# Linear attention and a gated MLP on one core: query features turned on VectorE, numerators for a whole batch as sixteen array tiles, front and order set anew

## The chip, the cores and the metric

The kernel runs on one core of one Trainium2 chip. The metric is the device time of one execution in microseconds (us). The engines of the core are TensorE (PE in the profile; PEld is its weight load), VectorE (DVE), ScalarE (ACT), GpSimd (POOL) and SyncE (SP), which only issues DMAs here.

## What is computed

Four batches of 1088 tokens, 4 heads of 32. `phi` makes 64 features from two projections onto 8 directions each; attention is linear in these features; its output, 128 values a token, goes through a two-layer MLP of width 2048.

```python
a, b = einsum('rd,bhsd->bhsr', S1, x), einsum('rd,bhsd->bhsr', S2, x)    # phi(x):
phi = einsum('bhsi,bhsj->bhsij', a, b).reshape(..., 64)
q_p, k_p = phi(q), phi(k)
kv = einsum('bhsf,bhsd->bhfd', k_p, v);  z = sum(k_p, axis=2)
num = einsum('bhsf,bhfd->bhsd', q_p, kv)
den = einsum('bhsf,bhf->bhs', q_p, z)[..., None] + 1e-06
x = (num / den) as [4352 tokens, 128]
h = x @ w_in                                   # 128 -> 2048
g = where(h >= 1, h, where(h <= -1, 0, (h + 1) ** 2 / 4))
out = g @ w_out                                # 2048 -> 128
```

## The kernel before, in words

**The MLP.** Tokens lie along the free dimension in 9 chunks of 512 (the last 256); the width of 2048 is cut into 16 blocks of 128. One chunk and one block make a *unit*, 144 in all (0 to 143). Units 0 to 31 weave chunks 0 and 1, four blocks at a time, because the weights still arrive; then each chunk's 16 blocks follow one another; the last two chunks are woven again. Values and weights are split into a rounded part and a rest (`x_hi`, `x_lo`, `wi_hi`, `wi_lo`, ...), so a product is three matmuls. A unit is, in PE, three matmuls into `h` (L619 to L621) and three into `acc` (L655, L656, L659); in ACT the half-square `s` in two passes (L630, L632); in DVE the clamp `g` (L635); then `g_hi`, either as a cast on ACT (L641) or as a second clamp on DVE (L635), by the share `HI_ACT`; and `g_lo`, a subtraction on POOL (L645). The weights come as doubles and are taken apart by `from_double` on ACT, POOL and DVE (`mag`, `hc`, `m`, L366 to L394), 512 columns at a time (`raw_i`, `raw_o`).

**The attention of a batch.** `keys` projects the keys of 9 tiles of 128 tokens (`abk`), copies (`ab`, ACT), multiplies to features (`kp`, DVE; one group on POOL), sums the denominators' vector (`z`, `zm`) and the 64 x 32 sums per head (`kv`), and turns those into `kvb`. `queries` goes in groups of three tiles (batch 0: 2, 2, 3, 2): project with the denominators' vector beside it (`abq`, L521), copy (`as`), `terms`, `den`, its inverse, `ap`, then the features `qp` (L543, DVE). PE turns each tile's features in two transposes of 128 x 128 into a bank `tp` (L553), ACT or DVE copies it to `qpT`, and PE gathers the numerators `nd` (L571) in tiles of 64 rows by 32 columns. `x_hi` and `x_lo` are taken from `nd`. All of these stand beside the units of earlier chunks. Batch 0 is the *front*: unit 0 needs its first four tiles.

**The order.** Every step has a due time, written by hand or by a formula on its unit's number; `Plan.run` plays the steps with estimated costs on in-order engines and a fixed number of buffers (8 PSUM banks, tag `ps`) and writes out one order for each engine. A matmul `warm` fills PE where the plan has nothing for it before time `WARM`. Each engine runs its order as written and waits where an operand is late. DMAs go through SP's queue, and a few through ACT's (`load` with `lands`).

Of the kernel before, what the change touches and what calls it, by code (L numbers as in the profile page):

```python
# [18 lines left out]
P = 128  # L19
# [3 lines left out]
FIRST = 32  # L23
# [5 lines left out]
ND = 0.115  # L29
TP = 0.109  # L30
I0 = -12.0
LATE = 4
Q2 = -4.0
Q3 = -2.0
I1 = 2.0
O1 = 6.0
KP_POOL = (2,)
O0 = -4.0
K_LANDS = (2.6, 3.1)
Q_RATE = 210e3  # L40
KVM = 0.8
LOADS = {1: (-4.0, 0.0, -2.0), 2: (11.0, 13.0, 12.0), 3: (54.0, 58.0, 56.0)}
HI_ACT = (0.8, 0.36)
# [21 lines left out]
class Step:  # L65


    def __init__(self, due, ways):
        self.due, self.ways = due, ways
        self.next = []  # L70
        self.start = self.taken = None
        self.mode = 1


class Plan:
# [3 lines left out]
    AHEAD = 8.0  # L79
    WAIT = 0.45  # L80
    EDGE = 2.0
    SWITCH = 0.095
    STAY = 3.0
# [38 lines left out]
    def run(self):  # L122
# [26 lines left out]
        while left or done:  # L149
# [13 lines left out]
            for e in engines:  # L163
# [51 lines left out]
                if e == "SP":  # L215
# [52 lines left out]
def tile_kernel(ctx: ExitStack, tc: tile.TileContext, qT, kT, v, S, w_in, w_out, outT):  # L268
# [14 lines left out]
                 ap=2, qp=2, qpT=4, kvm=1, kvb=2, zm=1, s=4, g=4, g_hi=6, g_lo=6, o=2)  # L283
# [28 lines left out]
    raw_i0 = Buf("raw", "raw_i0", [P, WC, 2], I32)  # L312
    k0 = Buf("k", "k0", [P, NTL, P])
    nc.gpsimd.memset(of(k0)[:, 3, :1], 0)
# [15 lines left out]
    x_hi = cst.tile([P, NT + 64], F32R, name="x_hi")  # L330
    x_lo = cst.tile([P, NT + 64], F32R, name="x_lo")
# [19 lines left out]
    def from_double(due, raw, raw_tok, n, tag, whole=None, whole_tok=None, hi=None, lo=None, toks=None):  # L351
# [10 lines left out]
        def m():  # L362
# [3 lines left out]
        plan.add(due, "ACT", act(n, False), lambda: nc.scalar.activation(of(mag), hw().bitcast(F32), AF.Abs),  # L366
                 r=[raw_tok], w=[mag])
# [29 lines left out]
    def weights(due, src, c, hi, lo, tag, due_load=None, lands=None):  # L397
        raw = raw_i0 if lands is not None else Buf("raw", f"raw_{tag}{c}", [P, WC, 2], I32)
# [14 lines left out]
    QLOAD = [range(0, 4), range(4, NTL)]  # L413
    QPART = [0, 0, 1, 1]
    loaded = {}

    def load_attn(b, due_k, due_q, due_v):
        kb = Buf("k", f"k{b}", [P, NTL, P]) if b else k0
        qb = Buf("q", f"q{b}", [P, NTL, P])
        vb = Buf("v", f"v{b}", [P, NTL, P])  # L420
        loaded[b] = kb, qb, vb
        for due, t, src in ((due_k, kb, kT), (due_q, qb, qT), (due_v, vb, v)):
            if b:
                load(due, src[b], t, P * NTL * P * 4)
            else:
                for i, grp in enumerate({0: GRP, 1: QLOAD, 2: [range(NTL)]}[[kb, qb, vb].index(t)]):
                    sl = slice(grp[0], grp[-1] + 1)
                    other = t is kb and i
                    load(-50 + i if other else (due if not isinstance(due, list) else due[i]) + 0.1 * i, src[b][:, sl], t,
                         P * len(grp) * P * 4, tok=t.part(i), view=lambda x, sl=sl: x[:, sl], lands=K_LANDS[i - 1] if other else None,  # L430
                         rate=Q_RATE if t is vb else 370e3 if t is qb and i else 190e3)

    def keys(b, d):
# [4 lines left out]
        late = 3.0 if front else 0.0  # L438
# [4 lines left out]
        for gi, grp in enumerate(groups):  # L443
            n = len(grp)
            kt = [kb.part(gi) if front else kb]
# [13 lines left out]
            pool = front and gi in KP_POOL  # L459
# [35 lines left out]
        for gi, grp in enumerate(groups):  # L495
# [3 lines left out]
        kvm = Buf("kvm", f"kvm{b}", [P, 2, F])  # L499
        copy_to(d(KVM) + late, lambda: of(kvm), lambda: of(kv)[:, :F].unsqueeze(1).broadcast_to([P, 2, F]), P, [kv], [kvm])  # L500
        plan.add(d(0.85) + late, "PE", 0.11, lambda: nc.tensor.transpose(
            out=of(kv)[:, P : 2 * P], in_=of(kvm).rearrange("p s f -> p (s f)"), identity=ident), r=[kvm], w=[kv]).mode = 0
        kvb = Buf("kvb", f"kvb{b}", [P, P])
        copy_to(d(0.9) + late, lambda: of(kvb), lambda: of(kv)[:, P : 2 * P], P, [kv], [kvb])
        return kvb

    def queries(b, kvb, dues):
        _, qb, _ = loaded[b]
        front = b == 0
        for gi, grp in enumerate(QGRP[b]):  # L510
# [32 lines left out]
            plan.add(d(0.4), "DVE", dve(m * F), lambda ap=ap, qp=qp, view=view, m=m, n=n: nc.vector.tensor_tensor(  # L543
                out=of(qp)[:, :n].rearrange("p t (h i j) -> p (t h) i j", h=H, i=R),
                in0=of(ap)[:, :m].unsqueeze(3).broadcast_to([P, m, R, R]),
                in1=view()[:, :, 1].unsqueeze(2).broadcast_to([P, m, R, R]), op=ALU.mult), r=[abc, ap], w=[qp])
# [39 lines left out]

    def x_tokens(kind, c0, n):
        out = []
        for b in range(B):
            for gi, grp in enumerate(QGRP[b]):  # L590
                lo = b * SEQ + grp[0] * P
                hi = b * SEQ + min(SEQ, (grp[-1] + 1) * P)
# [16 lines left out]
    AFTER = 3.6  # L609

    def unit(u):
# [14 lines left out]
        late = u >= len(units) - LATE  # L626
# [12 lines left out]
        share = 1.0 if late else HI_ACT[u >= FIRST]  # L639
# [30 lines left out]
    load(-30, S, s_raw, P * SC * 8, tok="s_raw", rate=94e3)  # L670
    load_attn(0, -29, [-28.5, -27], -27.5)
# [14 lines left out]
    kvb = keys(0, lambda f: -16 + 7 * f)  # L686
    queries(0, kvb, [lambda f: -9 + 4 * f, lambda f: -8.5 + 4 * f, lambda f: Q2 + 5 * f, lambda f: Q3 + 5 * f])
# [82 lines left out]
```

## Time and profile before

| | |
|---|---|
| three runs | 248.21 us median (248.18 to 248.82) |
| the profiled execution | 247.75 us, of which the span of instructions is 246.0 us |
| PE, PEld | 97%, 76% busy |
| ACT, DVE, POOL | 85%, 80%, 78% busy |
| chain that ended last | PE 68%, ACT 22%, DMA 3%, DVE 3% |
| TensorE clock granted | full speed throughout |

Read it with the end of the chain in mind: PE carries most of it, and ACT carries it up to about 69 us. A matmul's record overlaps the next one's, so what a matmul costs is read from the start of one to the start of the next.

### The profile page before, as it was taken

The numbers are of one execution on the slowest core, as the hardware profiler recorded it, in microseconds if no ns is written. First come the engines' busy times: TensorE is split into PE (matmuls) and PEld (weight loads), VectorE is DVE, ScalarE is ACT, GpSimd is POOL, SyncE is SP. The second block draws the span as 40 slices with busy tenths as digits, with TensorE's granted clock in tenths as the row PEclk, the third lists the DMA queues.
The fourth block names the chain that finished last, engine by engine and source line by source line (L and its number), as shares of the span: only waits on it lengthen the run. The fifth ranks groups of instructions, "written<-read, shape, count | busy, mean of one in ns | idle before, by whom it ended". The sixth has DMA issues, their size and how long they took to land.

```text
span 246.0 us, 5793 instructions
## 1 busy us (share of the span) xinstructions
PE 237.5 (97%) x2160; PEld 186.7 (76%) x2160; DVE 196.8 (80%) x386; ACT 209.8 (85%) x445; POOL 190.9 (78%) x175
## 2 busy tenths in 40 slices
PE   8699999999999999999999999999999999999994
PEld 3577768777858877878788787788778877888883
DVE  2499997499979767888779968787889799768873
ACT  2358999999998979977996689968996898889993
POOL 4234799999997768896797648895899488979991
PEclk9999999999999999999999999999999999999999
DMA  6972195300020100001000100001000100010001
GB/s 211 408 310 91 42 377 169 156 1 0 3 95 27 63 4 3 0 0 43 3 0 3 45 0 4 1 1 43 3 0 3 43 0 1 3 43 1 0 3 64
DMA packets 4779, 13.93 MB, mean 57 GB/s; under 512 B 528, under 2 KB 1168, under 8 KB 4752
## 3 DMA queue, kind: packets, MB, share of 16 engines
q1 hardware_dynamic: 4320, 12.65, 14.1%
q10 hardware_dynamic: 432, 0.92, 1.0%
q8 instruction: 17, 0.28, 0.5%
q14 instruction: 10, 0.08, 0.1%
HBM read 11.34 MB, written 2.23 MB: 55 GB/s over the span
## 4 chain that ended last, share of the span: by engine, by line
PE 68%; ACT 22%; DMA 3%; DVE 3%; issue 1%; POOL 0%; ACTq 0%; DVEq 0%; POOLq 0%
PE acc L659 11%; PE acc L655 10%; PE acc L656 10%; PE h L619 10%; PE h L621 9%; PE h L620 9%; ACT s L632 7%; ACT s L630 7%; ACT g_hi L641 5%; DMA raw_i<-in_w_in 3%; PE tp L553 2%; PE nd L571 2%; PE abq L521 2%; PE warm L292 1%; DVE g L635 1%
## 5 line engine op out<-in xcount | busy, mean ns | idle before, releaser
L645 POOL TENSOR_TENSOR g_lo<-g,g_hi 128x512 fp32r<-128x512 f32 (+1 forms) x140 | 171.8, 1250 | 34.9 <-DVE g_hi L635 16.2
L635 DVE SCALAR_TENSOR_TENSOR g<-h,s 128x512 f32<-128x512 f32 (+1 forms) x144 | 93.3, 657 | 31.8 <-ACT s L632 24.5
L630 ACT ACTIVATE s<-h 128x512 f32<-128x512 f32 (+1 forms) x144 | 79.8, 585 | 12.1 <-PE h L621 11.4
L632 ACT ACTIVATE s<-s 128x512 f32<-128x512 f32 (+1 forms) x144 | 86.5, 626 | 1.3
L619 PE MATMUL h<-x_hi,wi_hi 128*128 128x512 f32 (+1 forms) x144 | 56.1, 389 | 0.4 <-DVE g_hi L635 0.2
L655 PE MATMUL acc<-g_hi,wo_hi 128*128 128x512 f32 (+1 forms) x144 | 55.4, 386 | 0.1
L621 PE MATMUL h<-x_hi,wi_lo 128*128 128x512 f32 (+1 forms) x144 | 54.6, 379 | 0.0
L620 PE MATMUL h<-x_lo,wi_hi 128*128 128x512 f32 (+1 forms) x144 | 54.5, 379 | 0.0
L656 PE MATMUL acc<-g_hi,wo_lo 128*128 128x512 f32 (+1 forms) x144 | 54.4, 379 | 0.0
L659 PE MATMUL acc<-g_lo,wo_hi 128*128 128x512 f32 (+1 forms) x144 | 53.1, 397 | 0.0
L635 DVE SCALAR_TENSOR_TENSOR g_hi<-h,s 128x512 fp32r<-128x512 f32 (+1 forms) x76 | 50.0, 657 | 0.4 <-PE acc L656 0.2
L641 ACT CAST g_hi<-g 128x512 fp32r<-128x512 f32 (+1 forms) x68 | 40.9, 608 | 4.7 <-DVE g L635 3.8
L619 PEld LDWEIGHTS h<-x_hi,wi_hi 128*128 128x128 f32 x144 | 27.1, 188 | 7.0 <-DVE g_hi L635 1.1
L655 PEld LDWEIGHTS acc<-g_hi,wo_hi 128*128 128x128 f32 x144 | 27.1, 188 | 6.3 <-ACT s L632 0.5
L659 PEld LDWEIGHTS acc<-g_lo,wo_hi 128*128 128x128 f32 x144 | 26.6, 188 | 6.6 <-issue 1.2
L621 PEld LDWEIGHTS h<-x_hi,wi_lo 128*128 128x128 f32 x144 | 27.1, 188 | 5.2
L656 PEld LDWEIGHTS acc<-g_hi,wo_lo 128*128 128x128 f32 x144 | 27.1, 188 | 4.7
L620 PEld LDWEIGHTS h<-x_lo,wi_hi 128*128 128x128 f32 x144 | 27.1, 188 | 4.6
L543 DVE TENSOR_TENSOR qp<-ap,abq 128x768 f32<-128x768 f32 (+1 forms) x13 | 11.4, 887 | 0.1
L553 PE MATMUL tp<-ident,qp 128*128 128x128 f32 x72 | 11.2, 273 | 0.4 <-DVE qp L543 0.4
L462 DVE TENSOR_TENSOR kp<-ab,abk 128x1280 f32<-128x1280 f32 (+2 forms) x8 | 9.9, 1247 | 1.4 <-ACT ab L457 1.3
L553 PEld LDWEIGHTS tp<-ident,qp 128*128 128x128 f32 x72 | 8.9, 140 | 2.6 <-DVE qp L543 0.7
(75 smaller groups left out, 177.7 us busy)
## 6 DMA issues: line engine op xcount, KB each, us to landing
v<-in_v SPq DMA_DIRECT2D x4, 576.0 KB, 6.8
raw_o<-in_w_out SPq DMA_DIRECT2D x4, 512.0 KB, 5.0
outT<-o SPq DMA_DIRECT2D x8, 256.0 KB, 2.0
k<-in_kT SPq DMA_DIRECT2D x3, 576.0 KB, 5.2
q<-in_qT SPq DMA_DIRECT2D x3, 576.0 KB, 7.4
raw_i<-in_w_in SPq DMA_DIRECT2D x3, 512.0 KB, 4.7
raw_i<-in_w_in ACTq DMA_DIRECT2D x1, 512.0 KB, 7.6
k<-in_kT ACTq DMA_DIRECT2D x2, 192.0 KB, 3.9
```

The costliest lines, as they stand in the source:

```text
L553: nc.tensor.transpose(out=of(tp)[:, i * P : (i + 1) * P], in_=of(qp)[:, i, p * P : (p + 1) * P], identity=ident)
L619: nc.tensor.matmul(t[:, :n], lhsT=wi_hi[:, fj], rhs=x_hi[:, xs], start=True, stop=False)
L620: nc.tensor.matmul(t[:, :n], lhsT=wi_hi[:, fj], rhs=x_lo[:, xs], start=False, stop=False)
L621: nc.tensor.matmul(t[:, :n], lhsT=wi_lo[:, fj], rhs=x_hi[:, xs], start=False, stop=True)
L630: plan.add(u, "ACT", act(n), lambda: nc.scalar.activation(of(s)[:, :n], of(h)[:, :n], AF.Relu, bias=0.5, scale=0.5), r=[h], w=[s])
L632: plan.add(u, "ACT", act(n, False), lambda: nc.scalar.activation(of(s)[:, :n], of(s)[:, :n], AF.Square), w=[s])
L635: nc.vector.scalar_tensor_tensor(out=of(out)[:, :n], in0=of(h)[:, :n], scalar=1.0, in1=of(s)[:, :n], op0=ALU.max, op1=ALU.min)
L641: plan.add(u, "ACT", act(n, False), lambda: nc.scalar.copy(of(g_hi)[:, :n], of(g)[:, :n]), r=[g], w=[g_hi])
L645: plan.add(u, "DVE" if late else "POOL", dve(n) if late else pool_t(n), lambda: eng.tensor_tensor(out=of(g_lo)[:, :n], in0=of(g)[:, :n], i ...
L655: nc.tensor.matmul(of(acc)[:, :n], lhsT=wo_hi[:, fj], rhs=of(g_hi)[:, :n], start=first, stop=False)
L656: nc.tensor.matmul(of(acc)[:, :n], lhsT=wo_lo[:, fj], rhs=of(g_hi)[:, :n], start=False, stop=False)
L659: nc.tensor.matmul(of(acc)[:, :n], lhsT=wo_hi[:, fj], rhs=of(g_lo)[:, :n], start=False, stop=last)
```

## The change

In batches 1 to 3 VectorE turns the query features in blocks of 32 x 32 (`nc.vector.transpose` into `qt`), and PE computes the numerators of the whole batch in one step of 32 matmuls, each with 32 rows by 32 columns of the array (`gather16`, 9 or 8 tiles of tokens at once, four banks). `kvb` is laid out for that (two transposes of `kvm` for one). Batch 0 stays as it was. Beside it: some `kp` and `qp` steps go to POOL (`KP_POOL`, `QP_POOL`; ACT copies the second factor for these); some units of the first 48 keep `g` in PSUM and take `g_lo` on DVE and `g_hi` on ACT (`IN_PSUM`); `HI_ACT` has four shares, one for each 16 units up to unit 48 and one for the rest; the first loads are cut and queued anew (`FRONT`); the first step of the small matrix S's conversion goes to DVE; most due times are new numbers.

```diff
+ND16 = 1.45
-KP_POOL = (2,)
+KP_POOL = ((0, 2), (1, 0), (2, 1), (3, 1))
+IN_PSUM = (0.16, 0.17, 0.58, 0)
+QP_POOL = ((0, 2), (1, 0), (1, 2), (2, 0), (2, 1), (3, 1), (3, 2))
-HI_ACT = (0.8, 0.36)
+HI_ACT = (0.54, 0.61, 0.31, 0.35)
...
+    FRONT = {"k": ((0, KCUT, "SP", -29.0, 3.5), (KCUT, NTL, "ACT", -50.0, 3.5)), "v": ((0, NTL, "ACT", -45.0, 7.2),),
+             "q": ((0, 4, "ACT", -47.0, 5.6), (4, NTL, "SP", -26.5, 7.9))}
...
+        def turn():
+            for i in range(n):
+                nc.tensor.transpose(out=of(kv)[:, P * (i + 1) : P * (i + 2)], in_=flat(i), identity=ident)
...
+            if not front:
+                plan.add(d(0.5), "DVE", dve(n * H * F), lambda qp=qp, grp=grp, n=n: nc.vector.transpose(
+                    out=of(qt)[:, grp[0] : grp[-1] + 1].rearrange("p t f -> p (t f)"),
+                    in_=of(qp)[:, :n].rearrange("p t f -> p (t f)")), r=[qp], w=[qt.part(gi)])
+                continue
...
+        nds = [bank(f"nd{b}_{c}") for c in range(4)]
+        def gather16():
+            for k in range(2):
+                for h in range(H):
+                    for c, rows in enumerate(quarters):
+                        nc.tensor.matmul(
+                            of(nds[c])[quarters[h], : tiles[c] * D].rearrange("p (t f) -> p t f", f=D),
+                            lhsT=of(kvb)[rows, k * P + h * D : k * P + (h + 1) * D],
+                            rhs=of(qt)[rows, : tiles[c], h * F + k * D : h * F + (k + 1) * D],
+                            start=(k == 0), stop=(k == 1))
...
-        late = u >= len(units) - LATE
+        part = min(u // 16, 3)
+        late = u >= len(units) - LATE or int((u + 1) * IN_PSUM[part]) > int(u * IN_PSUM[part])
-        share = 1.0 if late else HI_ACT[u >= FIRST]
+        share = 1.0 if late else HI_ACT[part]
```

The written orders show three places. First SP's queue from its start, before: `s_raw`, the keys, queries and values of batch 0, then the weights (`raw_o`); `raw_i0`, the first block of `w_in`, is not in it, since ACT's queue issues it behind six tiles of keys.

```order
L346 DMA s_raw_93<-in_S 128x128
L346 DMA k0_71<-in_kT 128x384
L346 DMA q0_108<-in_qT 128x512
L346 DMA v0_111<-in_v 128x1152
L346 DMA q0_108<-in_qT 128x640
L346 DMA raw_o0_116<-in_w_out 128x1024
L346 DMA k1_123<-in_kT 128x1152
```

The same place of the change:

```order
L354 DMA s_raw_93<-in_S 128x128
L354 DMA k0_71<-in_kT 128x640
L354 DMA raw_i0_109<-in_w_in 128x1024
L354 DMA q0_103<-in_qT 128x640
L354 DMA raw_o0_114<-in_w_out 128x1024
L354 DMA k1_121<-in_kT 128x1152
L354 DMA v1_127<-in_v 128x1152
```

`raw_i0` is now third on SP's queue, behind five tiles of keys; ACT's queue has the other four tiles of keys, four of queries, and the values.

Second, PE around unit 0, before (the names: `h0` is unit 0, `tp0_3` the bank of turned features of batch 0, group 3, `nd0_3` its numerators, `abk1` the projected keys of batch 1, `z1` its sums):

```order
L619 MATMUL h0_438<-x_hi_91,wi_hi_87 128x512
...
L553 MATMUL tp0_3_0_481<-ident_66,qp0_3_468 128x128 x2
...
L571 MATMUL nd0_3_0_525<-qpT0_3_0_501,kvb0_335 32x128
...
L452 MATMUL abk1_0_538<-s_all_94,k1_123 32x64 x20
...
L452 MATMUL abk1_1_585<-s_all_94,k1_123 32x64 x16
L471 MATMUL z1_612<-ab1_0_571 32x32 x5
```

and in the change:

```order
L465 MATMUL abk1_0_356<-s_all_94,k1_121 32x64 x20
...
L589 MATMUL tp0_3_0_409<-ident_66,qp0_3_384 128x128 x2
...
L465 MATMUL abk1_1_421<-s_all_94,k1_121 32x64 x16
...
L607 MATMUL nd0_3_0_463<-qpT0_3_0_438,kvb0_380 32x128
...
L484 MATMUL z1_474<-ab1_0_396 32x32 x5
...
L484 MATMUL z1_474<-ab1_1_459 32x32 x4
...
L685 MATMUL h0_495<-x_hi_91,wi_hi_87 128x512
```

So group 3 of batch 0 and the first half of batch 1's keys moved ahead of unit 0, where PE had fillers.

Third, PE where the numerators of batch 1 are made, before (two of the six `tp` steps and the start of one of three gathers):

```order
L553 MATMUL tp1_0_0_1072<-ident_66,qp1_0_1059 128x128 x3
...
L553 MATMUL tp1_0_1_1085<-ident_66,qp1_0_1059 128x128 x3
...
L571 MATMUL nd1_0_0_1190<-qpT1_0_0_1097,kvb1_850 32x192
L571 MATMUL nd1_0_1_1192<-qpT1_0_0_1097,kvb1_850 32x192
L571 MATMUL nd1_0_0_1190<-qpT1_0_1_1118,kvb1_850 32x192
```

and in the change, where one step of 32 such matmuls stands between the units 23 and 24:

```order
L723 MATMUL acc0_636<-g_hi19_1046,wo_lo_90 128x512
L632 MATMUL nd1_0_1082<-qt1_846,kvb1_707 32x288
L632 MATMUL nd1_1_1084<-qt1_846,kvb1_707 32x288
L632 MATMUL nd1_2_1086<-qt1_846,kvb1_707 32x256
L632 MATMUL nd1_3_1088<-qt1_846,kvb1_707 32x256
...
L726 MATMUL acc0_636<-g_lo19_1070,wo_hi_89 128x512
L685 MATMUL h24_1131<-x_hi_91,wi_hi_87 128x512
```

The 18 transposes of the batch are gone from PE. The gathers of batches 2 and 3 stand in front of the units 61 and 92; the first units that read their results are 32, 64 and 96.

## Rows read from the trace of the kernel before

**Rows 1.** The page: span, busy time of each engine, and the chain that ended last by engine.

```profile
span 246.0 us, 5793 instructions
PE 237.5 (97%) x2160; PEld 186.7 (76%) x2160; DVE 196.8 (80%) x386; ACT 209.8 (85%) x445; POOL 190.9 (78%) x175
PE 68%; ACT 22%; DMA 3%; DVE 3%; issue 1%; POOL 0%; ACTq 0%; DVEq 0%; POOLq 0%
```

**Rows 2.** Busy time by stretch: from, to, length, then us (and instructions) of PE, PEld, DVE, ACT, POOL, the granted clock, DMA share, GB/s.

```profile
30.00:40.00 10.00, 9.90 (x118) 7.35 (x117) 9.80 (x17) 10.00 (x22) 9.47 (x9) 1.00 0.74 278
...
190.00:200.00 10.00, 10.00 (x66) 8.07 (x72) 8.10 (x14) 8.86 (x17) 5.84 (x6) 1.00 0.08 28
```

**Rows 3.** PE in order of time (start, length, line, operation): the first and the last of 23 unit matmuls of 512 columns that follow one another with nothing between.

```profile
90.72 0.40 PE L619 MATMUL h<-x_hi,wi_hi 128*128 128x512 f32 x1
...
95.75 0.39 PE L656 MATMUL acc<-g_hi,wo_lo 128*128 128x512 f32 x1
```

**Rows 4.** PE in order of time: three transposes between unit matmuls.

```profile
89.02 0.39 PE L659 MATMUL acc<-g_lo,wo_hi 128*128 128x512 f32 x1
89.25 0.49 PE L553 MATMUL tp<-ident,qp 128*128 128x128 f32 x3
89.49 0.47 PE L655 MATMUL acc<-g_hi,wo_hi 128*128 128x512 f32 x1
89.81 0.39 PE L656 MATMUL acc<-g_hi,wo_lo 128*128 128x512 f32 x1
```

**Rows 5.** PE in order of time: one gather between unit matmuls, and two gathers together; the profile counts each of the program's float32 matmuls twice.

```profile
71.75 0.39 PE L656 MATMUL acc<-g_hi,wo_lo 128*128 128x512 f32 x1
72.07 0.56 PE L571 MATMUL nd<-qpT,kvb 64*32 64x192 f32 x16
72.56 0.50 PE L659 MATMUL acc<-g_lo,wo_hi 128*128 128x512 f32 x1
72.89 0.39 PE L655 MATMUL acc<-g_hi,wo_hi 128*128 128x512 f32 x1
...
199.40 0.39 PE L656 MATMUL acc<-g_hi,wo_lo 128*128 128x512 f32 x1
199.72 0.88 PE L571 MATMUL nd<-qpT,kvb 64*32 64x192 f32 x32
200.52 0.50 PE L659 MATMUL acc<-g_lo,wo_hi 128*128 128x512 f32 x1
200.86 0.40 PE L619 MATMUL h<-x_hi,wi_hi 128*128 128x512 f32 x1
```

**Rows 6.** Groups by line: gathers of 192 columns over the whole span (busy us, mean ns of one).

```profile
L571 PE MATMUL nd<-qpT,kvb 64*32 64x192 f32 x136 | 5.1, 333 | 0.0
```

**Rows 7.** PE in order of time: projected keys of batch 2 between unit matmuls.

```profile
73.59 0.39 PE L656 MATMUL acc<-g_hi,wo_lo 128*128 128x512 f32 x1
73.91 0.77 PE L452 MATMUL abk<-s_all,k 128*32 128x64 f32 x40
74.61 0.73 PE L659 MATMUL acc<-g_lo,wo_hi 128*128 128x512 f32 x2
```

**Rows 8.** All engines in order of time, the front from the load of `raw_i0` on ACT's queue to unit 0.

```profile
2.33 0.45 ACTq L342 DMA_DIRECT2D raw_i<-in_w_in  x1
...
9.97 0.66 ACT L366 ACTIVATE magi<-raw_i 128x512 f32<-128x512 f32 x1 [2.45 <-DMA raw_i<-in_w_in]
10.54 0.31 ACT L457 COPY ab<-abk 128x192 f32<-128x192 f32 x1
...
13.54 0.20 DVE L530 TENSOR_TENSOR terms<-as,abq 128x64 f32<-128x64 f32 x1
...
20.13 0.48 PE L619 MATMUL h<-x_hi,wi_hi 128*128 128x512 f32 x1
21.11 0.60 ACT L630 ACTIVATE s<-h 128x512 f32<-128x512 f32 x1 [1.00 <-PE h L621]
```

**Rows 9.** DMA queues from 0 to 7 us: packets, MB (q1 is SP's, q10 is ACT's).

```profile
q1 hardware_dynamic: 561, 1.08, 45.6%
q10 hardware_dynamic: 327, 0.55, 22.0%
```

**Rows 10.** The group of ACT's casts `g_hi` between 20 and 76 us (units 0 to 31): count, busy us, mean ns of one, then idle time before.

```profile
L641 ACT CAST g_hi<-g 128x512 fp32r<-128x512 f32 x25 | 16.3, 663 | 0.6 <-DVE g L635 0.6
```

**Rows 11.** ACT in order of time: passes back to back (start to start gives what one takes from the engine), and the start of `s` of unit 32.

```profile
49.33 0.63 ACT L641 CAST g_hi<-g 128x512 fp32r<-128x512 f32 x1
49.84 0.66 ACT L632 ACTIVATE s<-s 128x512 f32<-128x512 f32 x1
50.37 1.10 ACT L630 ACTIVATE s<-h 128x512 f32<-128x512 f32 x2
...
76.53 0.60 ACT L630 ACTIVATE s<-h 128x512 f32<-128x512 f32 x1 [0.16 <-PE h L621]
```

**Rows 12.** Features on DVE (with what follows) and on POOL, and POOL's `g_lo`.

```profile
58.89 0.94 DVE L543 TENSOR_TENSOR qp<-ap,abq 128x768 f32<-128x768 f32 x1
59.75 0.68 DVE L635 SCALAR_TENSOR_TENSOR g<-h,s 128x512 f32<-128x512 f32 x1
...
11.30 1.51 POOL L462 TENSOR_TENSOR kp<-ab 128x768 f32<-128x768 f32 x1
...
L645 POOL TENSOR_TENSOR g_lo<-g,g_hi 128x512 fp32r<-128x512 f32 x128 | 163.5, 1298 | 34.9 <-DVE g_hi L635 16.2 <-ACT g_hi L641 12.6 <-PE h L621 2.1
```

More of the change, by code (lines that the diff above doesn't have):

```diff
@@ L22 @@
 WARM = 24.0
-FIRST = 32
 ABK = 0.16
@@ L214, in run @@
                                 b.held = False
-                if e == "SP":
+                if s.lands is not None:
+                    end = max(s.lands, now + 1.6)
+                    wire = max(wire, end - 0.6)
+                elif e == "SP":
                     wire = max(wire, now + 1.0) + lat
@@ L421, in load_attn @@
         loaded[b] = kb, qb, vb
-        for due, t, src in ((due_k, kb, kT), (due_q, qb, qT), (due_v, vb, v)):
+        for name, due, t, src in (("k", due_k, kb, kT), ("q", due_q, qb, qT), ("v", due_v, vb, v)):
             if b:
                 load(due, src[b], t, P * NTL * P * 4)
[L425 to L431, printed above, removed]
+                continue
+            for i, (a, e, eng, due, lands) in enumerate(FRONT[name]):
+                load(due, src[b][:, a:e], t, P * (e - a) * P * 4, tok=t.part(i), view=lambda x, a=a, e=e: x[:, a:e],
+                     lands=lands, eng=eng)
     def keys(b, d):
@@ L437, in keys @@
         tag = "h" if front else "at"
-        late = 3.0 if front else 0.0
+        late = FKV if front else 0.0
         z = bank(f"z{b}")
@@ L444, in keys @@
             n = len(grp)
-            kt = [kb.part(gi) if front else kb]
+            kt = [kb.part(i) for i in range(2) if (grp[0] < KCUT if i == 0 else grp[-1] >= KCUT)] if front else [kb]
             ab = bank(f"abk{b}_{gi}", tag)
@@ L585, in queries @@
                     r=[nds[k], ("xh", b, gi, k)], w=[("xl", b, gi, k)])
+        if front:
+            return
+        nds = [bank(f"nd{b}_{c}") for c in range(4)]
+        tiles = [-(-(SEQ - c * HR) // P) for c in range(4)]
+        def gather16():
[7 more added lines that the diff above has]
+                            start=(k == 0), stop=(k == 1))
+        plan.add(d(0.8), "PE", ND16, gather16, r=[kvb, *(qt.part(i) for i in range(len(QGRP[b])))], w=nds).mode = 3
+        for c in range(4):
+            m = tiles[c] * D
+            src = lambda c=c, m=m: of(nds[c])[:, :m].rearrange("p (t f) -> p t f", f=D)
+            dst = lambda x, c=c: x[:, b * SEQ + c * D : b * SEQ + c * D + tiles[c] * P].rearrange(
+                "p (t f) -> p t f", f=P)[:, :, :D]
+            copy_to(d(0.9), lambda dst=dst: dst(x_hi), src, m, [nds[c]], [("xh", b, c)])
+            plan.add(d(1.0), "DVE", dve(m), lambda src=src, dst=dst: nc.vector.tensor_tensor(
+                out=dst(x_lo), in0=src(), in1=dst(x_hi).bitcast(F32), op=ALU.subtract),
+                r=[nds[c], ("xh", b, c)], w=[("xl", b, c)])
     def x_tokens(kind, c0, n):
@@ L589, in x_tokens @@
         for b in range(B):
+            if b:
+                if b * SEQ < c0 + n and (b + 1) * SEQ > c0:
+                    out += [(kind, b, c) for c in range(4)]
+                continue
             for gi, grp in enumerate(QGRP[b]):
-                lo = b * SEQ + grp[0] * P
-                hi = b * SEQ + min(SEQ, (grp[-1] + 1) * P)
+                lo = grp[0] * P
+                hi = min(SEQ, (grp[-1] + 1) * P)
                 if lo < c0 + n and hi > c0:
```

130 lines of the change are left out of this document (75 added, 55 removed).

## The prediction, made blind

> **What bounds the kernel now.** I read the page first, then the stretches of ten microseconds, then PE in order of time. The page says that PE is busy 97% of 246.0 us and that the chain which ended last runs through PE for 68% and through ACT for 22% [rows 1]. The stretches say where: from 30 to 40 us ACT is busy all of the time, DVE and POOL 9.80 and 9.47 of 10.00, while at 190 to 200 us PE alone is full and POOL has 4 of 10 us free [rows 2]. Busy time says little of PE itself, since records overlap, so I took starts. Twenty-three unit matmuls with nothing between them start 22 steps apart in 95.75 - 90.72 = 5.03 us, 0.229 us each [rows 3]. Of the 144 units 128 have 512 columns and 16 have 256; with half the price for these that is 136 x 6 x 0.229 = 187 us of unit work. Unit 0 starts at 20.13 us [rows 8]. So 246.0 - 20.1 - 187 leaves about 39 us for the attention's matmuls beside the units, the waits, and the tail of some 4 us behind the last matmul. Everything that leaves PE's order after unit 0 is therefore worth its own time, as long as no other engine takes over; and everything that makes unit 0 earlier is worth its time too. Where another engine is as full as PE, in units 0 to 31, the smaller of two savings counts.
>
> **The front.** Today unit 0 waits for a chain that begins with the first block of `w_in`. It is issued at 2.33 us on ACT's queue and ACT stands still for it until 9.97; the copy of the last keys' projection stands behind on ACT, at 10.54; the first `terms` of the queries start at 13.54, and unit 0 at 20.13 [rows 8]. In the change the block is third on SP's queue, behind 64 KB and 320 KB; with its own 512 KB that is 0.92 MB. In the first 7 us SP's queue moved 1.08 MB and ACT's 0.55 MB [rows 9]. At the same split 0.92 MB is through at about 6.5 us; at equal shares of the two queues it needs 1.84 MB in all, 0.2 MB more than the 1.63 MB of these rows, and lands about 7.5. So ACT's first pass over it comes 2.5 to 3.5 us earlier, and with it the copy and the first `terms`; I take 3.2. From there to unit 0 it took 6.6 us. The change puts group 3 of batch 0 (another 0.6 us of features on DVE and its transposes) and the keys of batch 1 ahead of unit 0 and moves two conversion passes of DVE behind it; queued up by hand that gives 6.3 to 8 us, and I take 6.9. Unit 0 then starts near 17.2: **2.9 us** earlier, bounds 1.2 and 4.
>
> **PE in units 0 to 31.** Three transposes between unit matmuls: from 89.02 to 89.81 are 0.79 us, less two unit matmuls 0.33 us [rows 4]. A gather alone: 72.89 - 71.75 = 1.14 us, less two unit matmuls 0.68; two gathers together: 200.86 - 199.40 = 1.46, less two, 1.00 [rows 5]. Forty projections of keys: 74.61 - 73.59 = 1.02, less one, 0.79 [rows 7]. In this stretch the change takes away twelve transposes of batch 1 (four times 0.33), two gathers (twice 0.68), the 72 projections and sums of batch 1's keys (about 1.6), and group 3 of batch 0 (about 0.9), and puts the last half of batch 2's projections behind unit 32 (0.8): 6.0. It adds one gather of the new kind (next part, 1.4) and a second transpose of `kvm` (0.1). PE could be 4.5 us shorter here.
>
> **The new gather's price** no row shows. The program's 32 matmuls are 64 in the profile, four for each of sixteen tiles of the array, each of 288 or 256 columns. That tiles do work beside each other is seen: 136 gathers of 192 columns have a mean of 333 ns and together are busy 5.1 us, not 45 [rows 6]. Sixteen more of them cost 1.00 - 0.68 = 0.32 us [rows 5]: two more per tile of eight, 384 columns, 0.83 ns a column. Four times 272 columns then take 0.91, and with the fixed 0.36 of a gather 1.27 us. If the number of instructions sets it instead, sixteen more at 0.32 are 20 ns each and 64 give 0.36 + 1.28 = 1.64; the projections, 40 in 0.70 us [rows 7], show 17.5 ns. I take **1.4**, bounds 1.27 and 2.1 (the second is two gathers together, 1.00, taken twice). The Trainium skill, "TensorEngine Tiling (Array Packing)", section Instruction Overhead, gives every matmul an overhead of about 60 cycles; at 2.4 GHz that would be 25 ns, so 64 would take 1.6 us and a gather 1.96 by estimate, 1.7 us more over the three than my sum. The 17.5 ns of the projections lie below it, so I do not build on it.
>
> **ACT in units 0 to 31.** ACT goes from `s` of unit 0 at 21.11 to `s` of unit 32 at 76.53, 55.4 us [rows 8, 11], full all the way. Its order there has 25 casts `g_hi` now [rows 10] and 20 after, at 0.51 us from start to start [rows 11]: 2.6 less. Three copies of projected keys go (0.9, at 0.3 each), three of four copies of turned features (0.9), and one conversion pass moves each way. New are two copies for `kvb` (0.5), two more and longer `x_hi` (0.8) and the wider copies for POOL (0.2). Together **2.9 us** less. That is less than PE's 4.5, so ACT keeps the end of this stretch and I count 2.9. DVE and POOL are not let off either: in the same stretch DVE loses four clamps, three copies and a product or so and gains five `g_lo`, three turns and longer `x_lo`, which comes out near even; POOL loses five `g_lo` of 1.3 us and gains two `qp` of about 1.5 [rows 12]. Both need about 48 of the 52.5 us that ACT leaves, so they are covered, but thinly.
>
> **The turn on VectorE** has no row either. Its nearest is the product of 768 elements, which takes 59.75 - 58.89 = 0.86 us from the engine [rows 12]; it cannot be cheaper than half of that or, I assume, dearer than twice. Nine turns are 7.7 us, spread over three batches; in units 0 to 31 three of them at twice the price add 2.6 us and DVE stays below ACT. On PE's path a turn is late only where the gather of its batch waits; the orders put the gathers of batches 1, 2 and 3 eight, three and four units ahead of the first unit that reads them, with keys' sums between, some 5 us or more, against some 3 us for four `x_hi` and four `x_lo`. I cost the wait at nothing; if that cover goes, it is at most those 3 us a batch. The gather also needs four of eight banks at once; that leaves two or three for `h` for about 2 us, and I put 0.5 us into the range for it.
>
> **PE from unit 32.** PE alone sets the end [rows 2]. Away go 42 transposes, fourteen times 0.33 = 4.6, and seven gathers: two alone at 0.68, two pairs at 1.00 and 0.7, one beside other float32 work at 0.4, together 3.4. Added are two new gathers (2.8), two transposes of `kvm` (0.3) and batch 2's projections from the stretch before (0.8). Saved: 8.0 - 3.9 = **4.1 us**.
>
> **Sum.** 2.9 + 2.9 + 4.1 = 9.9 us. The profiled execution took 247.75 us, 1.75 beyond its span, so it would take 237.9; it lies 0.46 below the median of the three runs, and the forecast for the median is **238.0 us**, between 237.9 and 238.3. About 0.3% is what a measurement of this kernel can tell from no change.
>
> **The rivals.**
> PE decides units 0 to 31 as well. ACT's steps are estimates of throughput, and ACT had 1.4 us between its work (54.0 by start-to-start prices) and its stretch. Then 4.5 counts instead of 2.9, and with a front at its better bound (4) the time is about 235. For it: PE is at 9.90 of 10.00 beside ACT's 10.00 [rows 2], both full. Against: ACT has no idle time there, and no step of the change shortens its two passes a unit.
> The gather goes by instructions, at its upper bound of 2.1 us or by the skill's rule above at about 2: three times 0.7 more, 240. For it: from the start of a gather to the next matmul, 72.56 - 72.07 over 16, it is 31 ns an instruction [rows 5]; against it, that this holds the fixed part too.
> The front gives nothing: the two queues share otherwise, or the work put ahead of unit 0 fills what the load gave. 237.9 + 2.9 = 240.8.
> Four engines at over nine tenths wait for one another in units 0 to 31 and at the gathers, so that half of the gain is given back: 243.
> The sixteen tiles do not work beside each other but in turn, as sets of rows. One matmul of 272 columns holds its tile for 272 x 0.83 ns = 0.23 us; 64 of them in turn are 14.5 us, 13 more than counted, 39 for three gathers, and the time would be near 277. It decides against the change from 1.4 + 9.9 / 3 = 4.7 us a gather. Against it: the ninefold overlap of [rows 6], which needs both sets of rows and all four of columns at once.
>
> **How the numbers follow.** Forecast, 235.5 to 240: 0.62. PE decides and a better front, 232.5 to 235.5: 0.15. Gather by instructions: 0.07. No gain in front: 0.06. Engines waiting for one another, 241 to 246: 0.05. Tiles in turn: 0.04. No net change: 0.01. The range from 232.5 to 243 holds the first four and part of the fifth. Faster by over 0.3% is all but the last two and a little of the fifth: 0.93; within 0.3% 0.02; slower 0.05.
>
> **What would show it.** ACT's first pass over `raw_i0` at 6.5 to 7.5 us and unit 0 near 17.2. No `tp` behind batch 0, and nine turns of about 0.9 us on DVE. From the unit matmul before a new gather to the one behind it 1.6 to 1.7 us, two of which lie in PE's work after unit 32. `s` of unit 32 about 52.5 us behind that of unit 0, with ACT still full between, and PE without idle time from there to the end. I am wrong if unit 0 stays at 20, if a gather takes over 2.1 us, or if PE shows gaps in front of the units 32, 64 and 96, where `x_lo` would be late.

## The result, and the profile after

The changed kernel takes **240.15 us** (median of four runs, 240.06 to 241.36) against 248.51 of the kernel before beside it: a ratio of 0.967, with an interval of 0.962 to 0.971. The forecast was 238.0. The profiled execution is one of the four (240.06, span 238.4).

The sum by stages, with units counted by work done: the 192nd unit matmul closes as much work as units 0 to 31 hold.

| stage | before | after | gain | forecast |
|---|---|---|---|---|
| start to unit 0 | 20.13 | 20.90 | -0.8 | 2.9 |
| first to 192nd unit matmul | 58.2 | 54.6 | 3.7 | 2.9 |
| from there to the end | 167.7 | 162.9 | 4.8 | 4.1 |

So the front lost 0.8 us where 2.9 were forecast, and the other two stages gave 1.5 us more than forecast. The page and the stretches of after, which answer to [rows 1, 2] (50 to 60 us is new):

```profile
span 238.4 us, 5734 instructions
PE 229.9 (96%) x2133; PEld 181.7 (76%) x2133; DVE 193.0 (81%) x373; ACT 209.7 (88%) x441; POOL 189.3 (79%) x171
PE 63%; ACT 23%; DVE 4%; DMA 3%; issue 3%; POOL 2%; ACTq 0%; POOLq 0%; DVEq 0%
```

```profile
30.00:40.00 10.00, 10.00 (x68) 7.89 (x68) 10.00 (x21) 10.00 (x23) 9.26 (x9) 1.00 0.79 293
50.00:60.00 10.00, 8.92 (x55) 6.35 (x67) 10.00 (x20) 9.97 (x20) 9.98 (x9) 1.00 0.01 2
190.00:200.00 10.00, 10.00 (x47) 8.27 (x46) 8.01 (x13) 9.97 (x21) 10.00 (x9) 1.00 0.01 5
```

The columns are PE, PEld, DVE, ACT and POOL, then the granted clock, the share of DMA and GB/s. From 50 to 60 us DVE, ACT and POOL are full together, and PE has a us of ten free. From 190 to 200 us, where PE alone was full before, ACT and POOL are now as full as PE. The new gather and the turn, PE and DVE:

```profile
59.37 0.40 PE L723 MATMUL acc<-g_hi,wo_lo 128*128 128x512 f32 x1
59.69 1.59 PE L632 MATMUL nd<-qt,kvb 32*32 32x288 f32 x64
61.21 0.50 PE L726 MATMUL acc<-g_lo,wo_hi 128*128 128x512 f32 x1
```

```profile
L579 DVE STREAM_TRANSPOSE qt<-qp x9: 920/967/972, 42.3 to 164.9; 128x768 f32<-128x768 f32 x9
```

```profile
42.32 0.97 DVE L579 STREAM_TRANSPOSE qt<-qp 128x768 f32<-128x768 f32 x1
43.21 1.50 DVE L702 SCALAR_TENSOR_TENSOR g<-h,s 128x512 f32<-128x512 f32 x2
```

From unit matmul to unit matmul 61.21 - 59.37 = 1.84; less one unit matmul a gather takes 1.61 us. A turn takes 43.21 - 42.32 = 0.89 us from DVE. The front, ACT (idle time before a row in brackets) and the chain, which answer to [rows 8]:

```profile
6.58 0.66 ACT L375 ACTIVATE magi<-raw_i 128x512 f32<-128x512 f32 x1 [0.56 <-DMA raw_i<-in_w_in]
11.68 0.21 ACT L555 COPY as<-abq 128x64 f32<-128x64 f32 x1 [2.63 <-PE abq L547]
```

```profile
2.34 7.92 DMA v<-in_v
10.30 0.69 PE kv L505 x24
10.99 1.92 PE abq L547 x48
17.77 1.15 issue
```

The weights are there at 6.58 us, as forecast. But ACT then waits 2.63 us for `abq`. In PE's order `abq` stands behind `kv0`, which waits for the values (third on ACT's queue, landed at 10.26). TensorE's clock was granted at half, 1.2 GHz, from 10.56 to 13.97 us; the row of 11 to 12 us shows it (0.50). And PE stands 1.15 us for "issue", which is time in which it waits for nothing that the profile shows, in the middle of 32 equal projections:

```profile
11.00:12.00 1.00, 1.00 (x32) 1.00 (x28) 0.08 (x1) 0.21 (x1) 0.00 (x0) 0.50 1.01 410
```

```profile
17.36 0.41 PE L465 MATMUL abk<-s_all,k 128*32 128x64 f32 x11
18.92 0.53 PE L465 MATMUL abk<-s_all,k 128*32 128x64 f32 x21 [1.15 <-issue]
20.90 0.48 PE L685 MATMUL h<-x_hi,wi_hi 128*128 128x512 f32 x1
```

### The profile page after: what moved, and what is told of

The parts are those of the page before. It is cut to its first block, busy times and chain, and to the rows that moved or that the text cites. A ratio compares the mean times of both kernels' runs of the same rounds, so it can differ in the third digit from the quotient of the medians.

```text
span 238.4 us, 5734 instructions
## 1 busy us (share of the span) xinstructions
PE 229.9 (96%) x2133; PEld 181.7 (76%) x2133; DVE 193.0 (81%) x373; ACT 209.7 (88%) x441; POOL 189.3 (79%) x171
## 4 chain that ended last, share of the span: by engine, by line
PE 63%; ACT 23%; DVE 4%; DMA 3%; issue 3%; POOL 2%; ACTq 0%; POOLq 0%; DVEq 0%
PE acc L722 9%; PE acc L726 9%; PE h L685 9%; PE acc L723 9%; PE h L686 9%; PE h L687 9%; ACT s L697 8%; ACT s L699 8%; ACT g_hi L708 5%; DMA v<-in_v 3%; PE nd L632 2%; PE abq L547 2%; DVE g L702 2%; PE kv L505 1%; PE abk L465 1%
## 5 line engine op out<-in xcount | busy, mean ns | idle before, releaser
L712 POOL TENSOR_TENSOR g_lo<-g,g_hi 128x512 fp32r<-128x512 f32 (+1 forms) x126 | 153.9, 1247 | 33.9 <-DVE g_hi L702 14.2
L697 ACT ACTIVATE s<-h 128x512 f32<-128x512 f32 (+1 forms) x144 | 80.9, 593 | 8.4 <-PE h L687 7.0
L687 PE MATMUL h<-x_hi,wi_lo 128*128 128x512 f32 (+1 forms) x144 | 54.6, 379 | 0.0
L702 DVE SCALAR_TENSOR_TENSOR g_hi<-h,s 128x512 fp32r<-128x512 f32 (+1 forms) x74 | 48.1, 652 | 4.4 <-PE acc L723 3.9
L726 PE MATMUL acc<-g_lo,wo_hi 128*128 128x512 f32 (+1 forms) x144 | 51.2, 387 | 0.0
L708 ACT CAST g_hi<-g 128x512 fp32r<-128x512 f32 (+1 forms) x70 | 42.0, 611 | 1.8 <-PE acc L726 1.0
L712 DVE TENSOR_TENSOR g_lo<-g,g_hi 128x512 fp32r<-128x512 f32 (+1 forms) x18 | 11.1, 627 | 2.4 <-ACT g_hi L708 2.2
L573 POOL TENSOR_TENSOR qp<-ap,as 128x768 f32<-128x768 f32 x7 | 10.6, 1517 | 0.0
L475 POOL TENSOR_TENSOR kp<-ab 128x1024 f32<-128x1024 f32 (+2 forms) x4 | 7.8, 1960 | 1.7 <-ACT ab L470 1.7
L579 DVE STREAM_TRANSPOSE qt<-qp 128x768 f32<-128x768 f32 x9 | 8.6, 958 | 0.0
```

The source lines that it names most:

```text
L573: lambda a=a, ap=ap, qp=qp, view=view, m=m, n=n, eng=eng, pool=pool: eng.tensor_tensor(out=of(qp)[:, :n].rearrange("p t (h i j) -> p (t h) ...
L687: nc.tensor.matmul(t[:, :n], lhsT=wi_lo[:, fj], rhs=x_hi[:, xs], start=False, stop=True)
L697: plan.add(u, "ACT", act(n), lambda: nc.scalar.activation(of(s)[:, :n], of(h)[:, :n], AF.Relu, bias=0.5, scale=0.5), r=[h], w=[s])
L702: nc.vector.scalar_tensor_tensor(out=of(out)[:, :n], in0=of(h)[:, :n], scalar=1.0, in1=of(s)[:, :n], op0=ALU.max, op1=ALU.min)
L708: plan.add(u, "ACT", act(n, False), lambda: nc.scalar.copy(of(g_hi)[:, :n], of(g)[:, :n]), r=[g], w=[g_hi])
L712: plan.add(u, "DVE" if late else "POOL", dve(n) if late else pool_t(n), lambda: eng.tensor_tensor(out=of(g_lo)[:, :n], in0=of(g)[:, :n], i ...
```

## The experiments

All are edits of the changed kernel but one. `move(steps, behind)` moves steps in the written order after the plan has made it, so that nothing else is planned anew; `at(engine, tiles)` finds a step. The edits are shortened. Ratios are to the kernel before, run on the same chip; the change's was 0.967 (0.962 to 0.971).

**The late values: moved out of the way, or covered.**

```diff
+    move([at("PE", "kp0", "kv0", "v0")], at("PE", "abq0_3", "q0"))
```

> The change's kernel with one step moved in PE's written order: the first part of `kv` of batch 0 (24 records, the ones that wait for the values) goes behind the three `abq` steps of queries; all else stays as written. Theory A (unit 0 is late because `abq` stands behind a wait for the values, and PE's clock falls in that wait): `abq` starts at 9.1 us, when its operand is copied, instead of 10.74, and at full clock; the first `terms` at about 10.2 instead of 11.92; unit 0 at 19.0 to 19.4 instead of 20.90; whole time 1.5 to 1.9 us less than the change, near 238.5. Theory B (the work of batch 1 put ahead of unit 0, and the load of code seen as an issue gap, set unit 0): `terms` come earlier, unit 0 stays within 0.5 us of 20.9. Theory C (the engines of units 0 to 31 are full anyway): unit 0 comes earlier, the whole time does not.

Measured: 241.33 us, ratio 0.974 (0.971 to 0.977); the profiled execution 239.93, with full clock. `abq` starts at 10.18 (later than expected, since PE had waited 1.0 us for the keys in this execution), the first `terms` at 11.23, and unit 0 at 20.93: theory B. The stop only grew, and ended at the same time (18.96):

```profile
PE abk L465 <- issue: 1.9, 1, 1.9
```

```diff
+    i = order.index(at("PE", "kp0", "kv0", "v0"))
+    for _ in range(13):
+        order.insert(i, filler)          # warm, 128x256
```

> The change's kernel with 13 more fillers `warm` of 256 columns on PE ahead of the first `kv` step, so that PE works while it would wait for the values (8.8 to 10.3 us); nothing is moved. It takes the clock's share of theory A by itself. If the fall of the granted clock to half from 10.56 to 13.97 us follows from that wait and counts: the clock stays full, 48 `abq` take about 1.0 instead of 1.9 us, and unit 0 comes 1.0 to 1.4 us earlier, near 19.7. If DVE's chain of `terms`, `den` and `ap` sets the pace there anyway: clock full, unit 0 at most 0.5 us earlier. If the clock falls for another reason: still 0.5 from 10.5 us on, and no gain.

Measured: 241.47 us, ratio 0.974 (0.970 to 0.978). The clock was full from 8 to 20 us. Unit 0 still came later, at 22.16: now PE stopped for 2.2 us, 26 records earlier in the program and so ahead of more work, until 19.10; and the clock fell to half behind that stop (20.25 to 23.66).

```profile
PE tp L589 <- issue: 2.2, 1, 2.2
```

**Work of batch 1 taken from ahead of unit 0.**

```diff
+    late = [s for s in order[: order.index(at("PE", "h3"))] if names(s) & {"abk1_1", "ab1_1"}]
+    move(late, at("PE", "h3"))
```

> The change's kernel with the second half of batch 1's keys (`abk1_1`, its copy on ACT, its sums `z1`) moved from ahead of unit 0 to behind unit 3 on PE and ACT. Theory B (this work and the 1.15 us issue gap in the middle of it hold unit 0): unit 0 1.5 to 1.9 us earlier, near 19.2, and the issue gap goes with it or costs nothing. If the gap belongs to a place in time or in the program and not to this step, it opens ahead of another step before unit 0, and unit 0 gains 0.6 us at most. Theory A alone: 0.6 or less. The whole time by as much as unit 0, unless the keys of batch 1 then come late.

> Both moves together: the first part of `kv` behind the three `abq` steps, and `abk1_1` with its copy and sums behind unit 3. If theories A and B each hold a share: unit 0 at 17.2 to 17.8, the forecast of the sum (17.2), and the whole time 3 us less than the change, near 237. If one of them has all of it, the same as that one alone.

Measured: 243.35 us (ratio 0.981, 0.976 to 0.985) and 243.7 us (0.982, 0.978 to 0.986), both slower than the change. Unit 0 at 21.11 and 19.77. The stop did not go with `abk1_1`: it opened ahead of `nd`, until 19.17 and 18.60. With both moves unit 0 came 1.1 us earlier, and more than that was lost behind it: the first to the 192nd unit matmul took 59.5 and 58.8 us instead of 54.6. With both moves PE goes from the start of unit 3 to that of unit 4 in 6.7 us instead of 3.2, as the moved projections stand there and PE waits behind them:

```profile
PE nd L607 <- DVE kp L475: 1.0, 1, 1.0
PE z L484 <- ACT ab L470: 0.5, 1, 0.5
```

The clock was also at half for 3.4 us in that stretch (27.5 to 30.9 us), and for 5.0 in that of the other run, so the loss is not the moved keys' alone.

What the change and these four have in common is a count. The matmuls and weight loads that PE had started when it stopped (columns as above), first of the change, then with the fillers, then with both moves:

```profile
0.00:18.50 18.50, 15.16 (x347) 10.71 (x348) 11.48 (x37) 9.06 (x27) 8.76 (x23) 0.91 0.81 310
```

```profile
0.00:18.50 18.50, 15.81 (x348) 10.61 (x348) 11.52 (x37) 7.95 (x25) 9.11 (x23) 1.00 0.81 310
```

```profile
0.00:18.00 18.00, 14.13 (x347) 9.26 (x347) 11.92 (x37) 9.16 (x27) 9.33 (x24) 1.00 0.84 317
```

694 to 696 in all five (705 or 706 with PE's few other records): a place in the program, not a step. Unit 0 of the kernel before stands ahead of that place, behind 668 of these records; in the change it stands behind 844. The DMA records show loads of code in pieces of 16 KB, one for about 251 of these records (4266 over 17 loads):

```profile
q8 instruction: 17, 0.28, 0.5%
```

In the five, one starts at 16.2 to 16.7 us and takes 1.0 to 1.1; PE goes on 1.2 to 1.5 us after it ends. It starts as the burst of data thins out (DMA share 1.01 at 15 to 16 us, 0.77 the next, 0.09 the one after). Five more variants below keep the first loads as they are, and stop at the same place. In one of them (`IN_PSUM` 0 for units 16 to 31) PE comes there late, at 18.31 us, and then stands only 0.76: the time at which PE goes on stays, not the length of the stop.

```profile
19.07 0.53 PE L465 MATMUL abk<-s_all,k 128*32 128x64 f32 x21 [0.76 <-issue]
```

**The burst thinned.**

```diff
+    gate = [memset on POOL of one column of v1 and of q1]
+    move([at("SP", "v1"), at("SP", "q1")], at("POOL", "ab1_0", "kp1"))   # the gate between
```

> The change's kernel with the loads of batch 1's values and queries (1.15 MB) taken out of the burst of the first 16 us: on SP they go behind `raw_o1` and wait for two small writes of POOL into their buffers, behind its `kp1` (about 18.9 us). Nothing else moves. It asks what holds PE's third piece of code. In the traces so far PE stops at its record 705 (weight loads and matmuls counted) in the change and in each variant of its front, until 18.6 to 19.2 us, 1.2 to 1.5 us after a 16 KB load of code ends that starts at 16.2 to 16.7, just as the burst of data ends. Theory D (the load of code waits behind the data in the DMA queues): with the burst ending about 14 us the load of code starts by 15.2 at the latest, PE does not stop at record 705, unit 0 comes 1.1 to 1.4 us earlier (19.5 to 19.8) and so does the end. Theory S (the load of code has its own time): it still starts at 16.2 to 16.7, PE stops as before, unit 0 stays at 20.9.

Measured: **238.28 us**, ratio 0.960 (0.956 to 0.964). Theory D. From 15 to 18 us, first the change, then this run:

```profile
15.00:16.00 1.00, 1.00 (x50) 0.74 (x50) 0.86 (x3) 0.84 (x4) 0.00 (x0) 1.00 1.01 407
17.00:18.00 1.00, 0.77 (x15) 0.45 (x14) 0.97 (x5) 0.94 (x4) 1.00 (x1) 1.00 0.09 29
18.00:19.00 1.00, 0.08 (x5) 0.08 (x8) 0.96 (x3) 0.46 (x1) 1.00 (x1) 1.00 0.01 4
```

```profile
15.00:16.00 1.00, 1.00 (x51) 0.74 (x57) 0.86 (x4) 0.82 (x3) 0.00 (x0) 1.00 0.18 61
17.00:18.00 1.00, 1.00 (x44) 0.74 (x50) 0.96 (x5) 0.94 (x4) 1.00 (x1) 1.00 0.00 0
18.00:19.00 1.00, 1.00 (x44) 0.62 (x44) 0.97 (x4) 1.00 (x5) 1.00 (x2) 1.00 0.00 0
```

```profile
17.32 0.65 PE L465 MATMUL abk<-s_all,k 128*32 128x64 f32 x32
19.42 0.48 PE L685 MATMUL h<-x_hi,wi_hi 128*128 128x512 f32 x1
```

The load of code starts at 15.03 instead of 16.59, PE runs its 32 projections in one piece, and unit 0 starts at 19.42, 1.48 us earlier. The projections start within 0.04 us of each other in the two traces (17.36 and 17.32), so what they differ by from there is the stop. From unit 0 to the end are 217.4 us, as in the change (217.5).

```diff
+    gate([o1], pool[pool.index(kp) - 1], raw)                # raw_o1
+    gate([v1, q1], kp, loaded[1][2], loaded[1][1])
+    move([at("PE", "kp0", "kv0", "v0")], at("PE", "abq0_3", "q0"))
```

> The run with the thinned burst, with two things more: the third load of `w_out` that SP issues in the front (`raw_o1`, 512 KB) also leaves the burst (it waits for a small write of POOL ahead of `kp1`, about 15 us), and the first part of `kv` of batch 0 goes behind the three `abq` steps, as in the first of the experiments. If the late values in PE's queue do cost once the load of code no longer hides it: `terms` 0.7 us earlier, no stop at record 705, unit 0 at 18.5 to 18.9 instead of 19.42, the end 0.6 to 0.9 us earlier than with the thinned burst alone, near 237.5. If another chain (the keys of batch 1, DVE) holds unit 0 by then: unit 0 within 0.3 us of 19.4 and the same time.

Measured: **237.69 us**, ratio 0.959 (0.955 to 0.963), the lowest of all medians, though its interval covers that of the run before. The load of code starts at 13.65, PE does not stop there, the first `terms` start at 10.36 (12.23 with the burst alone), and unit 0 at 18.45. So the step behind the late values does cost, but behind the load of code it could not be seen. The run changed two things at once, and how the 0.97 us gained at unit 0 divide between them was not tried. One more stop, after the piece before (442 records, 11.43 us), is left:

```profile
PE kv L505 <- issue: 1.0, 1, 1.0
```

**The gather's price.**

```diff
+                        if k == 1: tiny()                # 32 columns into a free part of the bank
                         nc.tensor.matmul(of(nds[c])[...], ...)
+                        if k == 0: tiny()
```

> The change's kernel with 32 more matmuls of 32 columns in each of the three new gathers (64 more in the profile), on the same tiles of the array, into columns of the four banks that nothing reads. By columns (each tile of the array is held 0.83 ns a column, 128 columns more a tile): a gather goes from 1.6 to about 1.7 us, whole time plus 0.3. By instructions (20 to 25 ns each): from 1.6 to 2.9 to 3.2 us, whole time plus 2.6 to 4.5 (two gathers lie where PE alone sets the end, one where other engines are full).

Measured: 244.86 us, ratio 0.986 (0.982 to 0.990), 4.7 us more than the change. From the 192nd unit matmul to the end, with two gathers in it, it took 165.9 us instead of 162.9.

```profile
171.36 0.39 PE L731 MATMUL acc<-g_hi,wo_lo 128*128 128x512 f32 x1
174.71 0.50 PE L734 MATMUL acc<-g_lo,wo_hi 128*128 128x512 f32 x1
```

174.71 - 171.36 = 3.35, less one unit matmul, 3.12 us: 64 records of a ninth of the columns cost 1.51 us, nearly as much as the 64 of the gather. It goes by instructions, 24 to 25 ns each.

**The pace of units 0 to 31.** In the change ACT is busy 51.52 of the 51.78 us from `s` of unit 0 to `s` of unit 32 (before 54.65 of 55.42):

```profile
21.87:73.65 51.78, 50.46 (x420) 37.81 (x418) 49.15 (x93) 51.52 (x106) 44.89 (x39) 1.00 0.31 110
```

Setting `HI_ACT` or `IN_PSUM` and letting the plan order everything anew says little of what the edit itself is worth, as these two show:

> The change's kernel with the first two shares of `HI_ACT` at 0.8 as before: of 32 units about 26 have the cast `g_hi` on ACT instead of 20, and DVE six clamps less. If ACT sets the pace in units 0 to 31 (the sum's term): six times 0.51 us, 2.5 to 3 us slower than the change. If the four engines are equally full there: 0.5 to 1.5 slower. If DVE or POOL is the bound there: no slower, perhaps faster.

> The change's kernel with IN_PSUM 0 for units 16 to 31: two units less keep `g` in a bank and take `g_lo` on DVE; POOL has two more `g_lo` of 1.25 us. PE shows two stalls at 52.8 us (1.24) and 62.0 us (0.39) where `h` waits for DVE's `g_lo` to set a bank free. If these stalls are banks held by `g`: they go, and the whole time is 1 to 1.6 us less. If POOL is as full as the rest there: they come back as waits for POOL, and the time is the same or up to 2 us more.

Measured: 246.92 us (ratio 0.995) and 244.23 us (0.985). The first to the 192nd unit matmul took 61.4 and 58.9 us instead of 54.6, with another order of all engines; in the first, 6.8 us of it were at half clock, and the second took three units out of the banks, not two. So both were made again with the written order kept:

```diff
+            cast = lambda: nc.scalar.copy(of(g_hi)[:, :n], of(g)[:, :n]) if u in (2, 10, 15, 20, 25, 30) ...
-            plan.add(u, "DVE", dve(n), lambda: clamp(g_hi), r=[h, s], w=[g_hi])
+            plan.add(u, "DVE", dve(n), cast, r=[h, s], w=[g_hi])
```

> The change's kernel, its written order untouched, but six units of 0 to 31 (2, 10 and so on, every other one that clamps `g_hi` on DVE) cast it on ACT at the same place: ACT gets six times 0.51 us, DVE loses six times 0.60. If ACT alone sets the pace from unit 0 to 31, as the sum had it: 2.5 to 3.1 us slower. If the four engines are equally near: 0.5 to 2 slower. If DVE sets it: the same or faster.

Measured: 243.94 us, ratio 0.984 (0.979 to 0.989). The first to the 192nd unit matmul took 57.8 us, 3.2 more than the change; against the run with fillers, whose clock fell at the same place (55.3), 2.6 more. Six casts are 3.1. From `s` of unit 0 to `s` of unit 32 ACT was full again, and DVE had 9 us free:

```profile
23.24:78.21 54.97, 51.31 (x422) 38.34 (x421) 45.80 (x86) 54.70 (x112) 45.53 (x38) 1.00 0.30 104
```

ACT sets this stretch: it grew by 3.2 us and ACT's work by 3.2, though DVE lost more than ACT gained.

```diff
+        real = late and 16 <= u < 32     # g in SBUF, g_lo on POOL, at the same places
```

> The change's kernel, its written order untouched, but the units among 16 to 31 that keep `g` in a bank and take `g_lo` on DVE (three of them) keep it in SBUF and take `g_lo` on POOL, at the same places. Setting the share to 0 and letting the plan order all anew had cost 2 to 4 us, which said nothing of the banks. If PE's stalls at 52.8 (1.24 us) and 62.0 us (0.39), where `h` waits for DVE's `g_lo`, are banks held by `g`: they go, and the end comes 1 to 1.6 us earlier, less what POOL adds. If POOL is as full as the others there (three times 1.25 us more for it, three times 0.6 less for DVE): `acc` waits for POOL instead, and the time is the same or up to 3 us more.

Measured: 242.39 us, ratio 0.975 (0.970 to 0.980). PE's wait of 1.3 us for DVE's `g_lo` went, and one of 1.3 us for DVE's turn came in its place; the stretch took 56.3 us, 1.0 more than in the run with fillers, whose clock fell at the same place. The waits were not the banks' alone.

**The gather and the turn alone,** put into the kernel before:

> The kernel before with the gather and the turn of the change alone (turn on VectorE, sixteen tiles, `kvb` in two parts for batches 1 to 3); front, shares of ACT and POOL and nearly all due times as before, but the plan's look-ahead `AHEAD` 12 instead of 8, without which it finds no four free banks. By the sum: from unit 32 on 42 transposes (4.6) and seven gathers (3.4) go, two new gathers at the measured 1.6 and two `kvm` turns (0.3) come: 4.5 us less; before unit 32 ACT sets the pace and little comes, 0 to 1. So 243 to 244. If the waits for four banks at once or for late `x_lo` take it back: 246 or more.

Measured: 261.08 us, ratio 1.051 (1.048 to 1.055): slower, and far beyond both expectations. From the 192nd unit matmul to the end it took 176.5 us instead of 167.7, 10.2 of them at half clock; the third gather waits for the turn, and takes 5.3 us instead of 1.6:

```profile
PE nd L615 <- DVE qt L562: 2.7, 1, 2.7
```

The rest of the 13 us is not accounted for, and how much the look-ahead costs by itself was not tried. So the gather and the turn did not pay alone; that the due times and shares of the change make them pay is likely, and not shown.

## Why the prediction was right or wrong

The time lies in the forecast's range, and the kernel gained 7.7 us of the 9.9 in its span. That is in part luck: the front was wrong by 3.7 us, and the other two stages gave back 1.5 of it.

**The front** (2.9 forecast, 0.8 lost) failed at two steps, and unit 0 at 20.90 is one of the prediction's own signs of being wrong. The load was right (6.58 us, forecast 6.5 to 7.5). The first step is "and with it the copy and the first `terms`; I take 3.2": `terms` came at 11.92, 1.6 us earlier and not 3.2, though DVE was through with `raw_i0` at 10.21, since the values' place on ACT's queue and the step `kv0` ahead of `abq` were read past. The second is "From there to unit 0 it took 6.6 us ... I take 6.9": it took 9.0. The 220 records of batch 1 and group 3 ahead of unit 0 (with 44 records of fillers fewer) were priced as PE's time, but pushed unit 0 across a piece of code whose load is late while the data arrive. Without that stop, with the burst thinned, `terms` to unit 0 took 7.2 us, so the price itself was near. Thinning the burst gives back 1.5 us, thinning it more with the step moved 2.5; unit 0 at 18.45 is still 1.25 behind the forecast, and PE stands 1.0 in that run at 11.43, of which it was not tried how much reaches unit 0. The rival "the front gives nothing" (240.8) was the case: the work put ahead of unit 0 did fill what the load gave, as it said, but by the load of code, which it did not name.

**Units 0 to 31** (2.9 forecast, 3.7): the right bound, ACT, as the six casts show. ACT's work there fell by 3.1 us, and its `s` of unit 32 came 51.8 us behind that of unit 0 (52.5 forecast). PE's own work beside the units shrank by 4.7 (11.8 to 7.1 us; forecast 4.5), of which 1.1 came back as waits between unit matmuls.

**From unit 32** (4.1 forecast, 4.8): the gather is 1.61, not 1.4, which two of them pay with 0.4; yet the work beside the units fell from 18.4 to 13.6 us, 4.9. With what was added (two gathers 3.2, `kvm` 0.3, projections 0.8) about 9.2 us left, and not 8.0. The projections now stand in pieces of 72 (1.23 us, where 40 and 32 apart took 0.8 and about 0.7), which no term held; that is about half of the difference, and the rest stays open. The tail is half a us shorter, and 0.6 came back between the unit matmuls.

**The gather by instructions** was a rival, and holds in its mechanism: 64 at 24 to 25 ns and a fixed part of at most 0.1 us, 1.6 us. The Trainium skill, "TensorEngine Tiling (Array Packing)", section Instruction Overhead, gives every matmul about 60 cycles, by estimate 25 ns at 2.4 GHz; the gather agrees. The projections lie below it (72 in 1.23 us, 17 ns each); the 17.5 ns of [rows 7], on which the forecast leaned, are theirs, over all 128 rows, and not those of 32 x 32 tiles. The sum had 1.64 as its bound by instructions, near by luck, from a fixed part of 0.36 and 20 ns, and went towards the columns instead; its 2.1 and 1.96 added a fixed part that is not there.

**The turn** takes 0.89 us from DVE (0.86 forecast), and no gather waits for it in the change. PE has gaps not in front of units 32, 64 and 96, but at 52.8 us (1.24) and 62.0 (0.39).

## What to carry to other kernels

Count instructions as well as time ahead of the first work that matters: PE's code comes by DMA too, and while the first loads fill the queues it comes late. Hold back loads that nobody needs yet, even if the queues are free for them. Judge a change of shares or tiles under a planner with the written order kept: of the three runs whose order was planned anew two came out 7 and 4 us slower than the change and one 13 slower than the kernel before, and none of them tells the edit from the order.

## What the runs showed of the hardware

PE stopped at fixed counts of records (442 and 694 to 696, some 253 apart), until 1.2 to 1.5 us after a 16 KB load of code had ended. With the first loads as in the change, in ten kernels, the load for the second place began at 16.2 to 16.7 us, whether PE had started its 512th record at 13.0 or at 14.7; with the data thinned it began 0.7 to 0.9 us after that record (13.65 and 15.03 us). The load before it began in the middle of the data (9.87 us in the change, at a DMA share of 1.09), so full queues delay such a load and do not bar it. The Trainium skill, "Runtime: NRT & Kernel Launch", section Instruction fetch mechanics, says that code comes in blocks of 16 KiB and that the cost of crossing one is "mostly hidden". The size agrees; where PE stopped here the cost was 0.4 to 2.2 us.

The granted clock fell to half for 3.41 us in some executions and not in others of the same kernel: behind PE's wait at 8.8 to 10.3 us in the change, not behind one of 2.2 us at the same place before, and behind the stop at 17 us in some variants and not in others. In the eight runs of the first experiment the span was 238.2 us with the clock full throughout, 238.7 at a mean of 0.997, and 239.4 to 240.1 at 0.989 to 0.993.
